# Gate logits with stationary weights in four column quarters, v moved past them, and the result turned by VectorE

## The chip, the core and the metric

One NeuronCore of a Trainium2 chip. The metric is the device time of one execution in microseconds (us). An engine is called PE (TensorE's matmuls), PEld (its weight loads), DVE (VectorE), ACT (ScalarE), POOL (GpSimd) or SP (SyncE) in the profile. Runs of one batch share a chip and are compared with the same runs of the kernel before. A ratio and its 95% interval are against the kernel before in the same batch.

## The reference, cut to what matters

```python
B, H, S, D = 8, 8, 576, 64                       # batches, heads, positions, head size
attn = exp(scores + bias) / sum                  # causal
x = (attn @ v) -> (B, S, H*D)                    # 512 columns a token
logits = einsum('bsd,de->bse', x, w_gate)        # 8 experts
local  = einsum('bsd,de->bse', x, w_local)       # 1 more column
# a token takes its argmax expert, or keeps the one of the token before (local gate)
h = relu(x @ w1[e]);  out = p[e] * (h @ w2[e])   # 8 experts, 512 -> 1024 -> 512
```

The kernel does not wait for x to get the gate logits. It computes v times the gate weights (nine columns a head) for each pair of heads, puts the result beside v, and lets the value rows of the attention carry these columns along. The rows then give x, its logits and the softmax sum in one product.

## The kernel before

The attention loop has 32 iterations, one for each pair of heads. All matmuls are fp32. The parts that the change touches, with cuts marked:

```python
HW = DH + E + 1                 # 73
VW = 2 * HW + 2                 # 148: sum | logits, v of head 0 | v, logits of head 1 | sum
TAIL = 2 * VW                   # banks are PSUM banks of 512 columns
GATE = TAIL + TL
gates = banks[1][:, GATE : GATE + NB * 2 * (E + 1)].rearrange("p (c h e) -> p c h e", c=NB, h=2)

def tail_scores(n):
    for h in range(2):
        d = slice(DH * h, DH * h + DH)
        mm(banks[1][d, TAIL : TAIL + TL], lhsT=ins[n][1][:, TS:][:, d], rhs=ins[n][0][:, TS:], ...)

def gate_parts(n):              # v stationary, the weights (18 columns) moving
    m = P // 2
    for c in range(NB):         # 5 chunks of positions
        for j in range(0, P, m):
            mm(gates[j : j + m, c], lhsT=ins[n][2][:, c * P + j : c * P + j + m], rhs=wz[:, n % HP], ...)

def beside_v(n):
    v = ins[n][3]
    nc.vector.tensor_copy(v[:, :, 1 : E + 2], gates[:, :, 0])
    nc.vector.tensor_copy(v[:, :, VW - E - 2 : VW - 1], gates[:, :, 1])

def rows(n, g):                 # ... scores stationary, v moving; then the division by the sums
    ...
# one iteration of the loop
    scores(n, u); weights(n, piece); tail(n); seen_tail(n)      # cut
    rows(n - 1, 1)
    rows(n - 1, 0)
    tail_scores(n + 1)
    gate_parts(n)
    beside_v(n)
```

In the expert stage, two early blocks of x are turned on TensorE, `transpose(ps[:, c, :], x[:, 128 columns], ident)` four times a block.

## Time and profile before

| | before |
|---|---|
| time, median of 4 runs | 789.76 us (788.81 to 790.12) |
| PE busy | 98% of the span |
| clean iteration of the attention loop | 6.93 us |
| of it: 10 logit matmuls | about 0.57 us |

The page, the clean iteration, the chain and the timeline stand in the prediction below. A clean iteration is one in which PE doesn't stop and nothing but the loop's own work is issued to it. What remains is what the logits' group and its two copies look like in the groups by form. The columns are: line, engine, operation, output from inputs, partitions by columns, count | busy us, mean ns of one | idle time of the engine before them.

```profile
L370 PE MATMUL o<-wz,vt 128*64 128x18 f32 x640 | 24.7, 209 | 0.6 <-issue 0.6
L375 DVE COPY v<-o 128x45 f32<-128x45 f32 x32 | 6.4, 199 | 8.1 <-PE o L370 4.2 <-DMA v<-in_vx_dram 2.9 <-PE bank L972 0.7
L376 DVE COPY v<-o 128x45 f32<-128x45 f32 x32 | 6.2, 195 | 0.0
```

The logits are 640 rows, 20 an iteration, because an fp32 matmul shows as two passes. Their mean of 209 ns is latency, not cost: 20 of them start within 0.57 us.

### The profile page before, as it was taken

How to read it: one execution, taken by the hardware profiler on the slowest of the kernel's cores; microseconds unless marked ns; L12 is line 12 of the kernel's file. 1: busy time of each engine (PE TensorE's matmuls, PEld its weight loads, DVE VectorE, ACT ScalarE, POOL GpSimd, SP SyncE). 2: the span in 40 equal slices, each digit the busy share in tenths (PEclk: the TensorE clock that was granted, in tenths of full speed). 3: DMA queues.
4: the chain of work that ended last, by engine and by line, in shares of the span. 5: the costliest groups of instructions: out<-in, count | busy, mean ns of one | idle time of the engine just before them, and what ended most of it. 6: DMA issues, size and time to landing. Idle time of an engine off the chain costs nothing.

```text
span 798.9 us, 18230 instructions
## 1 busy us (share of the span) xinstructions
PE 783.0 (98%) x7078; PEld 561.8 (70%) x7078; DVE 338.4 (42%) x1228; ACT 237.0 (30%) x611; POOL 175.4 (22%) x329
## 2 busy tenths in 40 slices
PE   9999999999999989999999999999999999999996
PEld 8989888888888854853777547774577735676762
DVE  3234444454557649325462264522655226546000
ACT  5767766756664111111111111111111111111110
POOL 3422344455432241101210002101111011011001
PEclk9999999999999999999999999999999999999999
DMA  9485579877474389956999369993699946994001
GB/s 312 170 294 186 187 236 303 312 247 237 170 254 179 113 290 411 393 192 242 335 387 408 127 228 352 387 395 116 246 345 394 361 150 229 373 411 188 22 14 43
DMA packets 64145, 204.47 MB, mean 256 GB/s; under 512 B 8269, under 2 KB 8301, under 8 KB 64048
## 3 DMA queue, kind: packets, MB, share of 16 engines
q1 hardware_dynamic: 55008, 172.41, 60.2%
q0 software_dynamic: 8896, 30.47, 10.0%
q8 instruction: 58, 0.95, 0.5%
q14 instruction: 39, 0.32, 0.1%
q10 hardware_dynamic: 144, 0.33, 0.1%
HBM read 179.93 MB, written 23.76 MB: 255 GB/s over the span
## 4 chain that ended last, share of the span: by engine, by line
issue 59%; PE 30%; POOL 4%; DVE 2%; POOLq 1%; SPq 1%; another core or an unknown queue 1%; DMA 0%; DVEq 0%
PE o L408 13%; PE ps L330 11%; POOL out_dram L1249 2%; PE o L370 2%; POOL xg L1184 2%; PE hp L1231 2%; PE o L286 1%; POOLq L1159 1%; PE o L351 1%; SPq L808 1%; PE bank L947 1%; DVE xT L1088 0%; SPq L804 0%; DVE x L413 0%
## 5 line engine op out<-in xcount | busy, mean ns | idle before, releaser
L1088 DVE STREAM_TRANSPOSE xT<-xg 32x128 f32<-32x128 f32 x576 | 174.2, 302 | 173.3 <-PE hp L1231 97.1
L1244 PE MATMUL yp<-w,hT 128*128 128x512 f32 (+1 forms) x528 | 217.6, 595 | 0.0
L1231 PE MATMUL hp<-xT,w 128*128 128x256 f32 (+1 forms) x1088 | 193.0, 337 | 2.8 <-issue 2.5
L1231 PEld LDWEIGHTS hp<-xT,w 128*128 128x128 f32 x1088 | 172.2, 191 | 27.4 <-issue 11.0
L339 ACT ACTIVATE sc<-ps,bias 128x256 f32<-128x256 f32 (+3 forms) x448 | 156.5, 482 | 60.6 <-PE ps L330 58.6
L1244 PEld LDWEIGHTS yp<-w,hT 128*128 128x128 f32 (+1 forms) x528 | 90.7, 181 | 115.4 <-issue 114.5
L1249 POOL DMA_INDIRECT out_dram<-y,at_gate x38 | 38.5, 1012 | 439.9 <-ACT y L1248 425.4
L408 PE MATMUL o<-v,sc 128*64 128x74 f32 x3072 | 117.9, 229 | 3.1 <-issue 2.9
L408 PEld LDWEIGHTS o<-v,sc 128*64 128x64 f32 x3072 | 110.9, 136 | 11.8 <-issue 9.2
L1235 ACT ACTIVATE hT<-hp 128x512 f32<-128x512 f32 x68 | 40.4, 597 | 195.6 <-PE hp L1231 183.3
L1248 ACT ACTIVATE y<-yp,at_gate 128x512 f32<-128x512 f32 x38 | 26.1, 688 | 240.5 <-PE yp L1244 234.3
L345 POOL TENSOR_SCALAR_AFFINE_SELECT sc<-sc 128x256 f32<-128x256 f32 x160 | 66.5, 420 | 129.0 <-ACT sc L339 60.8
L330 PE MATMUL ps<-q,k 64*128 64x320 f32 (+2 forms) x768 | 92.3, 386 | 0.0
L330 PEld LDWEIGHTS ps<-q,k 64*128 64x128 f32 x768 | 69.6, 186 | 14.6 <-ACT r_v L957 0.6
L1244 PE MATMUL yp<-x,hT 128*128 128x512 f32 (+1 forms) x144 | 63.3, 594 | 0.0
L1222 DVE STREAM_TRANSPOSE hT<-x 32x256 f32<-32x256 f32 x64 | 27.9, 436 | 65.4 <-ACT x L1216 64.5
L410 DVE RECIPROCAL recs<-o 128x4 f32<-128x4 f32 x64 | 12.1, 189 | 92.0 <-PE o L408 80.3
L1231 PEld LDWEIGHTS hp<-xT,x 128*128 128x128 f32 x320 | 46.1, 191 | 5.8 <-issue 2.6
L1231 PE MATMUL hp<-xT,x 128*128 128x128 f32 (+1 forms) x320 | 50.1, 317 | 0.0
L1244 PEld LDWEIGHTS yp<-x,hT 128*128 128x128 f32 (+1 forms) x144 | 25.3, 178 | 26.2 <-issue 25.8
L1038 POOL DMA_INDIRECT x_rows<-x,r_slot_i x40 | 38.9, 973 | 9.3 <-issue 5.7
L413 DVE TENSOR_TENSOR x<-o,recs 128x292 f32<-128x292 f32 x64 | 34.5, 538 | 2.2
(163 smaller groups left out, 350.6 us busy)
## 6 DMA issues: line engine op xcount, KB each, us to landing
w<-in_w_dram SPq DMA_DIRECT2D x184, 512.0 KB
x<-in_w_dram SPq DMA_DIRECT2D x56, 512.0 KB
v<-in_vx_dram SPq DMA_DIRECT2D x32, 370.0 KB
vt<-in_vz_dram SPq DMA_DIRECT2D x32, 320.0 KB
k<-in_kz_dram SPq DMA_DIRECT2D x31, 320.0 KB
q<-in_q_dram SPq DMA_DIRECT2D x32, 288.0 KB
xg<-x_rows POOLq DMA_DIRECT2D x30, 293.0 KB
x_rows<-r_empty SPq DMA_DIRECT2D x6, 293.0 KB
```

Source lines behind the costliest of these rows:

```text
L330: mm(ps[:, h, at : at + z - a], lhsT=kb[d, c * P : c * P + P], rhs=qb[d, a:z], start=True, stop=True)
L339: nc.scalar.activation(scs[n, u][:, h, at : at + z - a], raw[u][:, h, at : at + z - a], Act.Exp, bias=bias[:, i : i + 1], scale=scale)
L345: nc.gpsimd.affine_select(out=x, in_=x, compare_op=Alu.is_ge, fill=0.0, base=0, pattern=[[0, 2], [1, P]], channel_multiplier=-1)
L408: mm(y, lhsT=w, rhs=x, start=start, stop=stop)
L413: nc.vector.tensor_tensor(x, y, rec.unsqueeze(3).to_broadcast([P, t1 - t0, 2, HW]), op=Alu.mult)
L1038: self.s.nc.gpsimd.indirect_dma_start(out=next(self.s.views)[:, :], out_offset=bass.IndirectOffsetOnAxis(ap=self.slot[:z, m : m + 1], axis=0),
L1088: self.nc.vector.transpose(self.xT[i][d : d + m, :, k * P + a * m : k * P + a * m + m], rows[a * m : a * m + m, :, X0 + d : X0 + d + m])
L1222: nc.vector.transpose(hT[i][d : d + m, :, a : a + m], x[a : a + m, :, d : d + m])
L1231: mm(y, lhsT=w[0][:, c, f : f + P], rhs=xT[i][:, c, :], start=(c == 0), stop=(c == DK - 1))
L1235: nc.scalar.activation(hT[i][:, g : g + per], ps, Act.Relu)
L1244: mm(ps[n * m : n * m + m, :], lhsT=hT[i][:, c, a : a + m], rhs=wn[:, c, :], start=(c == 0), stop=(c == FK - 1))
L1249: nc.gpsimd.indirect_dma_start(out=next(outs)[:, :], out_offset=bass.IndirectOffsetOnAxis(ap=at[i, k][:, 0:1], axis=0), in_=y[:, :], eleme ...
```

## The change

Intent: with v stationary, ten matmuls load 64 columns each to multiply 18. Turned round, the weights (32 columns, of which 18 are not zero) are stationary, and v's positions move past them. The array is used as four quarters of 32 columns, each with its own 32-position slices of the five chunks (5x32 = 160 moving columns), so four matmuls do what ten did. The result comes out with logits on partitions; VectorE turns it in 32x32 squares into a slot of 32 columns between the two heads' v.

```diff
+SLOT = 32
+VX = 2 * DH + SLOT + 2
+PARTS = slice(0, VW // 2), slice(VX - VW // 2, VX)
@@
-    TAIL = 2 * VW
-    GATE = TAIL + TL
+    scores_of_tail = banks[0][:, 3 * VW : 3 * VW + TL]
+    gates = banks[1][:, 2 * VW : 2 * VW + NB * SLOT].rearrange("p (c n) -> p c n", c=NB)
@@ def gate_parts(n):
-        m = P // 2
-        for c in range(NB):
-            for j in range(0, P, m):
-                mm(gates[j : j + m, c], lhsT=ins[n][2][:, c * P + j : c * P + j + m], rhs=wz[:, n % HP],
-                   start=True, stop=True)
+        m = P // 4
+        v = ins[n][2].rearrange("p (c n) -> p c n", c=NB)
+        for j in range(0, P, m):
+            mm(gates[j : j + m], lhsT=wz[:, n % HP], rhs=v[:, :, j : j + m], start=True, stop=True)
@@ def beside_v(n):
-        nc.vector.tensor_copy(v[:, :, 1 : E + 2], gates[:, :, 0])
-        nc.vector.tensor_copy(v[:, :, VW - E - 2 : VW - 1], gates[:, :, 1])
+        nc.vector.transpose(ins[n][3][:, :, 1 + DH : 1 + DH + SLOT], gates)
@@ the loop
             rows(n - 1, 1)
+            divide(n - 1, 1)
             rows(n - 1, 0)
         if n + 1 < NPAIR:
             tail_scores(n + 1)
+        if n:
+            divide(n - 1, 0)
@@ def product (x turned by TensorE in the experts)
-            self.nc.tensor.transpose(ps[:, c, :], x[:, 2 * c * HW + X0 : 2 * c * HW + X0 + P], self.ident)
+            for h in range(2):
+                self.nc.tensor.matmul(ps[h * DH : h * DH + DH, c, :], lhsT=rows[:, c, X0[h] : X0[h] + DH],
+                                      rhs=self.ident, start=True, stop=True)
... (cut: the layout of v and x in memory, the stores that follow it, the weights' slot, gx 5 -> 4)
```

The logits now take 160 columns of the second bank. With the rows' 296 and the tail's 64 that is 520, more than the bank's 512. So the tail's scores had to move to the first bank, and that bank's division had to move behind them.

More of the change, by code (lines that the diff above doesn't have):

```diff
@@ L33 @@
 VW = 2 * HW + 2
+SLOT = 32
+VX = 2 * DH + SLOT + 2
+PARTS = slice(0, VW // 2), slice(VX - VW // 2, VX)
 TOPS = ((0, None), (1, 2), (4, 3), (5, 6), (8, 7))
 PLAIN = ((0, 1), (2, 3), (4, 5), (6, 7), (8, None))
-X0 = E + 1
+X0 = 0, 2 * HW - DH
 XI = H * HW
@@ L197, in general @@
                     r0, z = b * S + t * P, min(P, S - t * P)
-                    nc.sync.dma_start(xb[:z, t, :XI].rearrange("p (a w) -> p a w", w=2 * HW)[:, :, X0 : X0 + P],
-                                      x_d[r0 : r0 + z, :].rearrange("p (a w) -> p a w", w=P))
+                    for h in range(2):
+                        nc.sync.dma_start(xb[:z, t, :XI].rearrange("p (a w) -> p a w", w=2 * HW)[:, :, X0[h] : X0[h] + DH],
+                                          x_d[r0 : r0 + z, :].rearrange("p (a w) -> p a w", w=P)[:, :, h * DH : h * DH + DH])
                 g = sort.group((b,), {b: xb})
@@ L252, in load @@
         ins[n] = [p_in.tile([P, S], F32, name="q"), *(p_in.tile([P, TS + 2 * TL], F32, name=x) for x in ("k", "vt")),
-                  p_vx.tile([P, NB, VW], F32, name="v")]
+                  p_vx.tile([P, NB, VX], F32, name="v")]
         for t, x, eng in zip(ins[n], (q[b][:, hp], kz[n], vz[n], vx[n]), (nc.sync, other, nc.sync, nc.sync)):
@@ L268, in attention @@
     load(2)
-    wz = keep.tile([P, HP, 2, E + 1], F32, name="wz")
+    wz = keep.tile([P, HP, SLOT], F32, name="wz")
     nc.gpsimd.memset(wz, 0.0)
@@ L273, in attention @@
         d = slice(h * DH, h * DH + DH)
-        for w, a, z in ((w_gate, 0, E), (w_local, E, E + 1)):
-            nc.gpsimd.dma_start(wz[d, :, h, a:z], w.rearrange("(a h d) e -> h d a e", h=2, d=DH)[h])
+        at = 0 if h == 0 else SLOT - E - 1
+        for w, a, z in ((w_gate, at, at + E), (w_local, at + E, at + E + 1)):
+            nc.gpsimd.dma_start(wz[d, :, a:z], w.rearrange("(a h d) e -> h d a e", h=2, d=DH)[h])
     seen = once.tile([P, TL], F32, name="seen")
@@ L350, in tail_scores @@
             d = slice(DH * h, DH * h + DH)
-            mm(banks[1][d, TAIL : TAIL + TL], lhsT=ins[n][1][:, TS:][:, d], rhs=ins[n][0][:, TS:], start=True, stop=True)
+            mm(scores_of_tail[d], lhsT=ins[n][1][:, TS:][:, d], rhs=ins[n][0][:, TS:], start=True, stop=True)
     def tail(n):
@@ L356, in tail @@
         i = tail_bias + n
-        nc.scalar.activation(sc, banks[1][:, TAIL : TAIL + TL], Act.Exp, bias=bias[:, i : i + 1], scale=scale)
+        nc.scalar.activation(sc, scores_of_tail, Act.Exp, bias=bias[:, i : i + 1], scale=scale)
     def seen_tail(n):
@@ L361, in seen_tail @@
         nc.vector.scalar_tensor_tensor(x, x, 3e38, seen, Alu.min, Alu.mult)
-    gates = banks[1][:, GATE : GATE + NB * 2 * (E + 1)].rearrange("p (c h e) -> p c h e", c=NB, h=2)
     def gate_parts(n):
-        m = P // 2
-        for c in range(NB):
-            for j in range(0, P, m):
-                mm(gates[j : j + m, c], lhsT=ins[n][2][:, c * P + j : c * P + j + m], rhs=wz[:, n % HP],
-                   start=True, stop=True)
+        m = P // 4
+        v = ins[n][2].rearrange("p (c n) -> p c n", c=NB)
+        for j in range(0, P, m):
+            mm(gates[j : j + m], lhsT=wz[:, n % HP], rhs=v[:, :, j : j + m], start=True, stop=True)
     def beside_v(n):
-        v = ins[n][3]
-        nc.vector.tensor_copy(v[:, :, 1 : E + 2], gates[:, :, 0])
-        nc.vector.tensor_copy(v[:, :, VW - E - 2 : VW - 1], gates[:, :, 1])
+        nc.vector.transpose(ins[n][3][:, :, 1 + DH : 1 + DH + SLOT], gates)
     def rows(n, g):
-        b, hp = divmod(n, HP)
-        if (b, "x") not in xs:
-            xs[b, "x"] = new_x(b)
         t0, t1 = COLUMNS[g]
@@ L391, in rows @@
                 y = ps[half * TL : half * TL + TL, t - t0]
-                last = i * TL == TS
-                if last:
-                    todo[half].append((y, scs[n, "tail"], v[:, NF], True, False))
                 cs = range(min(i // 2 + 1, NF))
-                for h in range(2):
-                    d = slice(h * VW // 2, (h + 1) * VW // 2)
+                for h, d in enumerate(PARTS):
+                    out = y[:, h * VW // 2 : (h + 1) * VW // 2]
+                    last = i * TL == TS
+                    if last:
+                        todo[half].append((out, scs[n, "tail"], v[:, NF, d], True, False))
                     for c in cs:
@@ L401, in rows @@
                         at += i * TL - a
-                        todo[half].append((y[:, d], scs[n, u][:, h, at : at + TL], v[:, c, d], not last and c == 0,
-                                           c == cs[-1] and (h == 1 or not last)))
+                        todo[half].append((out, scs[n, u][:, h, at : at + TL], v[:, c, d], not last and c == 0,
+                                           c == cs[-1]))
         while any(todo):
@@ L408, in rows, with divide @@
                     mm(y, lhsT=w, rhs=x, start=start, stop=stop)
+    def divide(n, g):
+        b, hp = divmod(n, HP)
+        if (b, "x") not in xs:
+            xs[b, "x"] = new_x(b)
+        t0, t1 = COLUMNS[g]
+        ps = banks[g][:, : (t1 - t0) * VW].rearrange("p (t w) -> p t w", w=VW)
         rec = recs[:, n, 2 * t0 : 2 * t1].rearrange("p (t h) -> p t h", h=2)
@@ L419, in logits @@
             pair = keep.tile([P, NF, HP, E + 1], F32, name="pair")[:m, : t1 - t0]
-            nc.vector.tensor_tensor(pair, part[:, :, :, : E + 1], part[:, :, :, 2 * HW - E - 1 :], op=Alu.add)
+            nc.vector.tensor_tensor(pair, part[:, :, :, DH:HW], part[:, :, :, HW : HW + E + 1], op=Alu.add)
             nc.vector.tensor_reduce(lg[:m, b * NB + t0 : b * NB + t1, :], pair.rearrange("p t a e -> p t e a"),
@@ L1088, in squares @@
                 self.nc.vector.transpose(self.xT[i][d : d + m, :, k * P + a * m : k * P + a * m + m],
-                                         rows[a * m : a * m + m, :, X0 + d : X0 + d + m])
+                                         rows[a * m : a * m + m, :, X0[d // DH] + d % DH :][:, :, :m])
     def product(self, i, k, n, x, ps):
@@ L1094, in product @@
         ps = ps.rearrange("p (c n) -> p c n", c=DK)
+        rows = x[:, :XI].rearrange("p (c w) -> p c w", w=2 * HW)
         for c in range(DK):
-            self.nc.tensor.transpose(ps[:, c, :], x[:, 2 * c * HW + X0 : 2 * c * HW + X0 + P], self.ident)
+            for h in range(2):
+                self.nc.tensor.matmul(ps[h * DH : h * DH + DH, c, :], lhsT=rows[:, c, X0[h] : X0[h] + DH], rhs=self.ident,
+                                      start=True, stop=True)
         self.nc.vector.tensor_copy(self.xT[i][:, :, k * P : k * P + P], ps)
@@ L1132, in experts @@
     ps_r = pool("ps_r", 3, space=PSUM)
-    gx = gx or pool("gx", 5)
+    gx = gx or pool("gx", 4)
     ws, xg = (ready["w"], ready["x"]) if ready else ({}, {})
@@ L1321 @@
     kz, vz = (_np.zeros((NPAIR, 2, DH, TS + 2 * TL), _np.float32) for _ in range(2))
-    vx = _np.zeros((NPAIR, P, NB, VW), _np.float32)
+    vx = _np.zeros((NPAIR, P, NB, VX), _np.float32)
     for h in range(2):
@@ L1327 @@
         x = v[:, h::2].reshape(NPAIR, S, DH)
-        some = vx[:, :, :, h * (VW // 2) :][..., : VW // 2]
-        some = some[..., E + 2 :], some[..., 0], some[..., :DH], some[..., VW // 2 - 1]
-        some = some[2 * h : 2 * h + 2]
+        some = vx[..., (1, VX - 1 - DH)[h] :][..., :DH], vx[..., (0, VX - 1)[h]]
         some[0][:, :, :NF] = x[:, :TS].reshape(NPAIR, NF, P, DH).transpose(0, 2, 1, 3)
```

## The prediction

> **What bounds the kernel now.** I read the page's busy shares first, then the busy time by stage, the costliest groups, the order of work inside one iteration of the attention loop, and last the list of waits.
>
> ```profile
> PE 783.0 (98%) x7078; PEld 561.8 (70%) x7078; DVE 338.4 (42%) x1228; ACT 237.0 (30%) x611; POOL 175.4 (22%) x329
> ...
> L408 PE MATMUL o<-v,sc 128*64 128x74 f32 x3072 | 117.9, 229 | 3.1 <-issue 2.9
> ```
>
> TensorE is busy for 98% of the span and no other engine for half of it. The change touches the first 256 us, the attention loop of 32 iterations (one per pair of heads). One undisturbed iteration, from the windows view:
>
> ```profile
> 63.77:70.70 6.93, 6.93 (x149) 6.29 (x147) 2.04 (x8) 5.00 (x15) 2.04 (x5) 1.00 0.61 198
> ```
>
> The columns after the length are the busy times of PE, PEld, DVE, ACT and POOL, then clock and DMA. PE is busy for all 6.93 us, ACT for 5.00, DVE and POOL for 2.04. So in a clean iteration a PE microsecond saved is a microsecond saved. What an iteration's PE time consists of, from the chain of work in order of time:
>
> ```profile
> 42.05 2.79 PE ps L330 x24
> 44.84 3.42 PE o L408 x95
> 48.25 0.05 PE o L351
> ...
> 48.43 0.55 PE o L370 x19
> 48.98 2.98 PE ps L330 x24
> ```
>
> Scores (L330) take 2.79 us, the value rows (L408) 3.4, the tail's scores (L351) 0.1 and the logit parts (L370, the target of this change) about 0.57. Their ends and starts, from the timeline of PE around the logits:
>
> ```profile
> 62.96 0.23 PE L408 MATMUL o<-v,sc 128*64 128x74 f32 x1
> 63.01 0.23 PE L351 MATMUL o<-q,k 128*64 128x64 f32 x2
> 63.06 0.20 PE L370 MATMUL o<-wz,vt 128*64 128x18 f32 x1
> 63.08 0.22 PE L351 MATMUL o<-q,k 128*64 128x64 f32 x1
> 63.11 0.74 PE L370 MATMUL o<-wz,vt 128*64 128x18 f32 x19
> 63.77 0.54 PE L330 MATMUL ps<-q,k 64*128 64x320 f32 x2
> ```
>
> An fp32 matmul shows as two matmul rows and two weight loads (10 in the source, 20 here). From the last tail matmul's start (63.08) to the first scores matmul (63.77) pass 0.69 us: this stretch is what the change rewrites. A row's printed length (0.2 us) is latency; successive starts give the cost. The 20 logit passes start over 0.57 us in two column halves, 10 per half, so 57 ns per pass of only 18 moving columns: they are held by the loading of 64 stationary columns, not by streaming.
>
> **Rates that I use.** The page's groups by form give the streaming rate and an example of switching the array's shape:
>
> ```profile
> L1244 PE MATMUL yp<-w,hT 128*128 128x512 f32 x432 | 189.2, 595 | 0.0
> 359.57 0.59 PE L1244 MATMUL yp<-w,hT 128*128 128x512 f32 x1
> 360.10 0.65 PE L1214 MATMUL hp<-w,xT 128*64 128x512 f32 x2
> ```
>
> 189.2/432 = 438 ns per pass of 512 columns, or 0.84 ns a column in steady steps of 0.43 us. From the full array to column halves the step is 0.53 us, so a change of shape costs about 0.10 us. And the first two matmuls of the halves (x2) span 0.65 us together, one alone being about 0.64: both halves stream at once, although the second follows the two passes of the first in program order. The halves work independently of each other.
>
> **What the Trainium skill says.** "TensorEngine Tiling (Array Packing)", Key Properties: changing the tiling mode drains TensorE, and tiles load and multiply independently; the trace agrees, with the 0.10 us and the paired starts. Its tables list 128 by 32 as four tiles; no row of the kernel before shows four at once with fp32. "TensorE: Matmul & The Clock Gate", LDWEIGHTS: loading costs columns/1.2 ns whatever the rows, so 53 ns for 64 columns (trace: 57 per pass) and, as an estimate from that page, 27 ns for 32. The same page, Measured speedup vs the span model, gives 2.38x for three column tiles; whether that carries to fp32 passes is the main uncertainty. "PSUM — Partial Sum Buffer", PSUM bank collisions: two engines must not use one bank and quadrant together, so dependencies are kept by bank; the trace has such a wait, of the tail's scores for the division that reads other columns of the same bank:
>
> ```profile
> PEld o L351 <- DVE x L413: 1.7, 6, 0.3
> ```
>
> **The change, part by part.**
>
> (1) Logits. Removed per iteration: 10 matmuls (20 passes, 64 stationary columns, 18 moving). Added: 4 matmuls (8 passes, 32 stationary columns in four column quarters, 5x32 = 160 moving). If the quarters run at once, each does two passes of 160 x 0.84 = 135 ns. Counting from the last tail matmul: its own streaming of 64 columns 0.055, a new change of shape (halves to quarters) 0.10, one exposed load 0.027, two passes 0.27, stagger of the starts 0.02, then the change of shape to the scores 0.10 that was paid before as well: 0.57 us against 0.69. I take 0.13 us saved per iteration, times 31 full iterations: -4.0 us. The instructions fall by far more than the time: the new moving columns and the extra change of shape eat most of it.
>
> (2) Value rows. The tail's matmul of 148 columns becomes two of 74, since the heads' columns are no longer adjacent. In the first group that half of the array has now 16 matmuls of 74 instead of 14 and one of 148; the other half has 16 already. Same columns streamed: 0 us.
>
> (3) VectorE. Two copies of 128x45 (about 0.2 us each) become one 128x160 transpose. The existing 128-element transposes take 302 ns; I estimate 0.35 us for 160 columns. Its result is needed one iteration later, after 2.79 us of scores: 0 us on the path.
>
> (4) Tail's scores go from the second bank to the first, and the division of the first bank comes after them. The wait of 1.7 us in six iterations moves to the logits, some 0.3 us later (tail matmuls and a change of shape lie between), about as long as the longest such wait. Each of those iterations also loses the overlap of tail and logits. Most of it goes: -1.2 us.
>
> (5) Experts. Two blocks of x are turned on TensorE by four transposes each, between matmuls of the first layer:
>
> ```profile
> 263.49 0.60 PE L1096 MATMUL bank<-ident,xg 128*128 128x128 f32 x4
> 263.92 0.60 PE L1231 MATMUL hp<-xT,w 128*128 128x256 f32 x2
> ```
>
> 263.49 to 263.92 in this timeline, so 0.44 us a block. They become 8 ordinary fp32 matmuls with two passes of 128 columns, in two column halves: 4 x 2 x 0.109 = 0.87 us, plus two changes of shape and exposed loads of about 0.3. That is +0.7 us a block, +1.4 us in all, on a PE that has no gap there. The expert stage's VectorE transposes keep their shape and count.
>
> (6) Transfers. v grows from 148 to 162 columns, 370 to 405 KB per iteration. DMA's share in a clean iteration is 0.61 and loads are issued three iterations ahead: 0.
>
> Sum: -4.0 - 1.2 + 1.4 = -3.8, from 790.0 to about 786.2 us.
>
> **Rivals.**
>
> *Quarters do not run four at once.* For it: the trace shows only two fp32 streams together. If two quarters share, the passes take 4 x 135 = 0.54 us instead of 0.27 and each iteration loses 0.14: 31 x 0.14 = +4.3, with (4) and (5) about 794.5. If all eight passes are serial, 1.08 us, each loses 0.68: some +21 us, 811. Against it: the two halves show no loss at all from sharing. I give the first 10%, the second 3%.
>
> *Quarters do not drain after halves.* If only the row side of the shape matters, the extra 0.10 us falls away: 3 us better, 783. For it, nothing in the trace: all visible changes of shape cost it. 15%.
>
> *The saving is swallowed by a wait that takes its place.* Iterations 13 to 30 are longer than 6.93 us (up to 8.5); there PE stops inside the rows while GpSimd issues the scatters, by 0.2 to 0.6 us at a time. These stops are put down to "issue", not to a semaphore of ACT or GpSimd. If they are latency from scores to rows through ACT and GpSimd, up to half of the saving in those iterations goes, 1.5 us. Against it: in them ACT still waits for the scores. If they are instructions arriving late, fewer PE instructions (20 of nearly 300 per iteration) help slightly. The same holds for a stop of about 3 us near 287 us, with a low clock after it (0.73 in that window), where ACT stands still: a shift of timing can make it larger or smaller by two or three microseconds. That widens the range both ways.
>
> *VectorE becomes the bound, or the expert stage does not start earlier.* VectorE has 4.9 us free per clean iteration. The expert stage's second weights land by 263 us and are first needed near 271: 8 us of slack. I give neither weight.
>
> **Range and chances.** Centre 786.2. Three microseconds either way cover the change of shape, the moved wait and the stops; the two-at-once rival lies outside above. 80% range 781.5 to 791. Faster by over 2% needs 774.2 or less, four times the expected gain: 0.02. Slower by over 2% needs 805.8, only the serial rival: 0.04. Within 2%: 0.94.
>
> **What will show it.** In the profile after: logit rows of 128*32 and 128x160, 256 in all, with four starts within some 20 ns and the next four about 0.135 us on; a gap of 0.57 us between the last tail matmul and the first scores matmul; a clean iteration of about 6.80 us; one 0.35 us transpose per iteration; no wait of the tail's scores for the division; 1.1 us per turned block in the experts. Wrong if the quarters' starts come one pair at a time (6.93 or more per iteration), if the gap falls to about 0.47 (no drain), or if the clean iterations gain and the end of the attention loop, now at 255 us, does not move by 5 us.

## The result, and the profile after

| | before | after |
|---|---|---|
| median | 789.76 us (788.81 to 790.12, 4 runs) | 784.06 us (783.42 to 784.55, 4 runs) |
| ratio | | 0.9929, 95% interval 0.9912 to 0.9946 |

Executions over 1.5% slower than the fastest of the same kernel are left out of the means. Ratios are the mean time of one kernel's runs over that of the other's runs of the same rounds, so they are not quite the ratio of the medians. (In the experiments they come out when the first round, which was profiled, is left out.) The change is 0.7% faster, inside the class "within 2%".

The busy shares on the page of the changed kernel:

```profile
PE 773.0 (99%) x6782; PEld 546.2 (70%) x6782; DVE 339.0 (43%) x1196; ACT 237.2 (30%) x611; POOL 176.2 (23%) x329
```

Its clean iteration in the windows view:

```profile
62.64:69.44 6.80, 6.80 (x140) 5.87 (x137) 2.08 (x7) 5.00 (x15) 2.04 (x5) 1.00 0.68 199
```

PE has 296 rows fewer and still fills the iteration; the iteration is 0.13 us shorter (6.930 to 6.796 from the records' starts). The groups by form of the logits and of the turning:

```profile
L374 PE MATMUL o<-vt,wz 128*32 128x160 f32 x256 | 15.7, 311 | 0.0
L377 DVE STREAM_TRANSPOSE v<-o 128x160 f32<-128x160 f32 x32 | 10.9, 342 | 2.8 <-DMA v<-in_vx_dram 2.8
```

256 rows in place of 640, and one turning of 342 ns in place of two copies of 199 and 195 ns. The timeline around them (start us, length us):

```profile
62.01 0.29 PE L356 MATMUL o<-q,k 128*64 128x64 f32 x3
...
62.23 0.48 PE L374 MATMUL o<-vt,wz 128*32 128x160 f32 x8
62.36 0.20 DVE L416 RECIPROCAL recs<-o 128x6 f32<-128x6 f32 x1 [0.72 <-PE o L356]
62.64 2.86 PE L335 MATMUL ps<-q,k 64*128 64x320 f32 x24
63.12 0.34 DVE L377 STREAM_TRANSPOSE v<-o 128x160 f32<-128x160 f32 x1
```

PE goes from the tail's scores (L356) to the logits (L374) to the next scores (L335) without a stop. The last tail matmul of the three starts at 62.08, so the stretch that the prediction counted is 0.56 us, against 0.69 before. The division of the first bank (L416) now waits for the tail's scores (L356), on VectorE, which has time. The turning ends at 63.46, two microseconds before PE leaves the scores. Each record of the eight logit passes has a start:

```
us: 62.231 62.238 62.245 62.251 | 62.391 62.398 62.405 62.411
```

Four start within 20 ns. The records don't name the quarter, but a quarter's pass of 160 columns takes 0.135 us, so these four are in four quarters and stream at once. The second passes follow 0.160 us later, not the 0.135 us that the prediction expected; the 0.025 us are about the one exposed weight load of its sum. The experts' turned block:

```profile
250.38 1.09 PE L1107 MATMUL bank<-ident,xg 128*64 128x128 f32 x16
251.40 3.72 PE L1243 MATMUL hp<-xT,w 128*128 128x256 f32 x16
```

From its start to the next layer's start 1.02 us pass, against 0.44 before; the work on both sides of it loses another 0.2 to the changes of shape.

**The profile of before was of a bad execution.** Its execution took 800.54 us, ten more than the timed runs (1.49% above the fastest of them), so its end of attention (255 us) can't be held against 242 us here. It shows stops of this kind in the rows of iterations 13 to 30 (timeline of PE):

```profile
234.47 0.63 PE L408 MATMUL o<-v,sc 128*64 128x74 f32 x10 [0.35 <-issue]
```

And it has a stretch near 287 us in which PE works for 3.55 of 6 us at a mean granted clock of 0.73 (windows view):

```profile
286.00:292.00 6.00, 3.55 (x6) 1.70 (x6) 2.95 (x20) 1.57 (x3) 0.96 (x1) 0.73 0.63 193
```

The first experiment therefore took a second profile of the same kernel.

### The profile page after: what moved, and what is told of

Its sections match the earlier page's. It is cut to its first block, busy times and chain, and to the rows that moved or that the text cites. A ratio compares the mean times of both kernels' runs of the same rounds, so it can differ in the third digit from the quotient of the medians.

```text
span 782.4 us, 17629 instructions
## 1 busy us (share of the span) xinstructions
PE 773.0 (99%) x6782; PEld 546.2 (70%) x6782; DVE 339.0 (43%) x1196; ACT 237.2 (30%) x611; POOL 176.2 (23%) x329
## 4 chain that ended last, share of the span: by engine, by line
issue 58%; PE 32%; POOL 5%; DVE 2%; POOLq 2%; DMA 1%; DVEq 0%
PE o L406 14%; PE ps L335 11%; POOL out_dram L1261 2%; POOL xg L1196 2%; PE hp L1243 2%; PE o L374 2%; PE o L291 1%; POOLq L1171 1%; DMA x_rows<-x,r_slot_i 1%; PE o L356 1%; PE bank L956 0%; DVE xT L1097 0%; POOL x_rows L1047 0%; PE bank L1107 0%; PE bank L981 0%
## 5 line engine op out<-in xcount | busy, mean ns | idle before, releaser
L406 PE MATMUL o<-v,sc 128*64 128x74 f32 x3072 | 113.6, 228 | 0.8 <-issue 0.8
L406 PEld LDWEIGHTS o<-v,sc 128*64 128x64 f32 x3072 | 108.8, 136 | 8.1 <-issue 4.3
L335 PE MATMUL ps<-q,k 64*128 64x320 f32 (+2 forms) x768 | 92.5, 386 | 0.1
L335 PEld LDWEIGHTS ps<-q,k 64*128 64x128 f32 x768 | 68.9, 186 | 20.0 <-issue 4.8
L416 DVE RECIPROCAL recs<-o 128x4 f32<-128x4 f32 x64 | 12.1, 189 | 87.0 <-PE o L406 63.1
```

The source lines that it names most:

```text
L335: mm(ps[:, h, at : at + z - a], lhsT=kb[d, c * P : c * P + P], rhs=qb[d, a:z], start=True, stop=True)
L406: mm(y, lhsT=w, rhs=x, start=start, stop=stop)
```

## The experiments

### Both kernels again: before_again, after_again

No edit; the two kernels as they are.

> The kernel before once more, with a second profile. Ratio 1.000. The profile in hand spans 798.9 us although the timed runs take 790: if its stops inside the rows (iterations 13 to 30), the waits of the tail's scores and the stop near 287 us belong to that one execution, this profile spans about 788 us and most of them are gone; if they belong to the kernel, it spans 799 again with the same stops. Clean iterations 6.93 us either way.

> The changed kernel once more, for a tighter ratio: 0.993, some 5.6 us. Sum known from the traces so far: 31 iterations x 0.134 us saved = -4.2, turning of x in the experts +1.4, so -2.8; the other -2.8 is open. Clean iterations 6.80 us again.

Measured: before 789.07 us (787.24 to 790.26, ratio 1.0004, interval 0.9990 to 1.0017); after 783.71 us (783.42 to 784.68, ratio 0.9933, interval 0.9919 to 0.9946). The expectation for before held: the profiled execution is now 787.24 us, with a span of 785.5 us and a clock of 1.00 in both windows below. Up to 252 us the bad profile had 13 stops of PE of over 0.15 us; up to 243 us this one has two, 0.52 us at 57.0 and 0.66 us at 242.3. Windows of before up to the first expert layer, and from there to the end:

```profile
0.00:246.15 246.15, 243.08 (x4836) 217.89 (x4836) 111.66 (x414) 164.27 (x494) 105.11 (x241) 1.00 0.74 243
246.15:785.50 539.35, 532.57 (x2243) 341.14 (x2243) 226.56 (x816) 72.53 (x117) 69.57 (x88) 1.00 0.72 268
```

The same of after:

```profile
0.00:241.99 241.99, 239.00 (x4516) 204.67 (x4516) 112.81 (x382) 164.27 (x494) 105.17 (x241) 1.00 0.75 252
241.99:782.50 540.51, 533.99 (x2267) 341.97 (x2267) 226.50 (x816) 72.51 (x117) 69.53 (x88) 1.00 0.72 267
```

So clean against clean, attention gains 4.2 us, the experts lose 1.2 us (539.35 to 540.51), and 3.0 us remain. The timed medians of that batch differ by 5.45 us (789.16 over nine runs of before, to 783.71), the fastest runs by 3.61 (787.03 to 783.42). The runs of before spread over 3 us and those of after over 1.3. A typical run of before takes 1.9 us more than its profiled one (787.24), a typical run of after 0.5 us less than its own (784.17); these 2.4 us of the gain are in neither profile, and no kept profile shows a typical run of before.

### The tail's scores moved, nothing else: tail_moved

```diff
-    TAIL = 2 * VW
-    GATE = TAIL + TL
+    scores_of_tail = banks[0][:, 3 * VW : 3 * VW + TL]
+    GATE = 2 * VW
...
+            divide(n - 1, 1)
             rows(n - 1, 0)
...
             tail_scores(n + 1)
+        if n:
+            divide(n - 1, 0)
```

> The kernel before with part 4 of the change alone: the tail's scores in the first bank, the division of the first bank after them; logits as before. Theory (the moved wait supplies the open 2.8 us): 1.5 to 3 us faster, ratio 0.9962 to 0.998, no wait of the tail's scores for the division, clean iterations still 6.93 us. Rival (the open part comes from fewer TensorE instructions to fetch, 20 of 300 per iteration): ratio 1.000.

Measured: 790.34 us (787.94 to 790.66), ratio 1.0010, interval 0.9997 to 1.0024. The theory fell: the move gains nothing by itself. Its clean iteration, in the windows view:

```profile
64.01:70.94 6.93, 6.93 (x149) 6.29 (x147) 2.04 (x8) 4.99 (x15) 2.03 (x5) 1.00 0.63 195
```

It is that of the kernel before to the hundredth. The waits of the tail's scores for the division are absent here, but they are absent in the second profile of before as well. They belonged to the bad execution, not to the kernel.

The move even has a small price, in the list of waits: the scores' weight loads wait for the routing's ranks (`r_rank`), which VectorE works out after the divisions. The three lines are of before_again, tail_moved and the changed kernel (us in total, times, longest):

```profile
PEld ps L330 <- DVE r_rank L1006: 0.5, 2, 0.3
...
PEld ps L330 <- DVE r_rank L1014: 1.3, 4, 0.4
...
PEld ps L335 <- DVE r_rank L1015: 1.6, 4, 0.5
```

Counted from one first scores matmul to the next, with the first iteration as 0, iterations 13, 21, 25 and 29 of tail_moved are each 0.13 us longer than those of before_again.

### The same turned product in two halves: halves

The weights stand in a slot of 96 columns with zeros on both sides, so that a 64-column half takes two accumulating matmuls, one for each of its quarters. All else is as in the changed kernel.

```diff
-    wz = keep.tile([P, HP, SLOT], F32, name="wz")
+    wz = keep.tile([P, HP, 3 * SLOT], F32, name="wz")
...
-            mm(gates[j : j + m], lhsT=wz[:, n % HP], rhs=v[:, :, j : j + m], start=True, stop=True)
+            first = j % (2 * m) == 0
+            some = wz[:, n % HP, SLOT:] if first else wz[:, n % HP, : 2 * SLOT]
+            mm(gates[j // (2 * m) * 2 * m :][: 2 * m], lhsT=some, rhs=v[:, :, j : j + m], start=first, stop=not first)
```

> The changed kernel with the logits' weights in two column halves (64 stationary columns, the other 32 of them zero, two accumulating matmuls of 160 columns per half): as many instructions as the quarters, no change of shape after the tail, but each half streams four passes of 160 columns. Theory (the gain comes from four streams at once): from the last tail matmul to the first scores matmul about 0.71 us instead of 0.56, clean iterations 6.95 us, 31 x 0.15 = 4.7 us slower than the changed kernel, about 788.7, ratio to the kernel before 0.999. Rival (the gain comes from fewer instructions): as fast as the changed kernel, ratio 0.993.

Measured: 788.87 us (788.78 to 789.63), ratio 0.9999, interval 0.9986 to 1.0013; the expected time and ratio held, and the rival fell, since halves has as many rows of PE as the changed kernel (6782) and gains nothing. The logits in the timeline:

```profile
62.66 0.76 PE L376 MATMUL o<-vt,wz 128*64 128x160 f32 x8
```

The clean iteration in the windows view:

```profile
63.36:70.34 6.99, 6.99 (x138) 6.15 (x137) 2.08 (x7) 4.99 (x15) 2.03 (x5) 1.00 0.65 198
```

The same number of logit matmuls, the same columns moved, two at a time: 6.99 us (expected 6.95), longer than before, and 0.75 us from the last tail matmul to the first scores matmul (expected 0.71). In this form, turning the operands round does not gain by itself; the gain is that four stream at once. Also, from the first tail matmul to the first logits pass 0.235 us here and 0.329 in the changed kernel: going from halves to quarters costs about 0.09 us.

### Each logits matmul two and three times: doubled, thrice, thrice_mixed

The result stays right, since each overwrites the same value.

```diff
-        for j in range(0, P, m):
+        for j in [j for j in range(0, P, m) for _ in range(2)]:      # doubled: 0,0,1,1,2,2,3,3
+        for j in [j for j in range(0, P, m) for _ in range(3)]:      # thrice:  0,0,0,1,1,1,...
+        for j in [j for _ in range(3) for j in range(0, P, m)]:      # thrice_mixed: 0,1,2,3,0,1,2,3,...
```

> The changed kernel with each of the four logits matmuls issued twice, the result the same. If four quarters stream at once, each quarter has four passes of 0.14 us instead of two: 0.28 us per iteration, 32 x 0.28 = 9.0 us, so 792.7 us, with the narrow spread of the changed kernel (about 1 us over its runs). If the quarters were served in turn, 8 more passes of 0.14: 36 us, 820. Theory for the open 2.4 us (the number of TensorE instructions brings stops that vary from run to run): with 16 more instructions per iteration it has nearly as many as the kernel before, so runs spread over 3 us and the median is near 795.

> The changed kernel with each of the four logits matmuls issued three times: 0.56 us per iteration, 17.9 us, 801.6 us if only streaming counts; if the number of TensorE instructions brings stops, more than the kernel before has now, so some 3 us above that and a wide spread.

> The changed kernel with each of the logits' four matmuls issued three times, as in the earlier run that came to 827.2 us, but with the quarters taken in turn (0,1,2,3,0,1,2,3,0,1,2,3) instead of each quarter's three together. If the order in which the quarters are issued is what kept them from overlapping there, each group of four passes adds 0.146 us as in the doubled run (0.292 us for two groups), so four groups more add 0.58 us an iteration: clean iteration 7.38 us, 783.7 + 31 x 0.58 = 801.8 us (800 to 803), and the four quarters' first passes start within 0.02 us. If it is the number of passes of the stage, the iteration stays at 8.2 us and the time at 827 us.

Measured: doubled 792.80 us (792.33 to 794.11, ratio 1.0056); thrice 827.20 us (827.15 to 827.82, ratio 1.0489); thrice_mixed 802.32 us (801.75 to 802.39, ratio 1.0149). The first came in where streaming puts it, and not where the theory of the instruction count did (795 us and a spread of 3 us; it was 1.8). The second missed both expectations by 23 to 26 us, and the third, which was made to find out why, came in at the sum for an overlap of four. Starts of the logit passes in one iteration, in us, from the records of each trace:

```
doubled       63.972 .986 .999 64.012 | 64.132 .146 .159 .172 | 64.268 ... | 64.404 ...     (16 starts in 0.47 us)
thrice        63.956 64.116 .252 .257 .387 .417 .523 .553 .559 .659 ... 65.428 65.564       (24 starts in 1.61 us)
thrice_mixed  58.966 .973 .979 .986 | 59.126 .133 .139 .146 | 59.262 ... | 59.398 ... (24 starts in 0.72 us)
```

The timeline shows the same as one row of each. Thrice first, then thrice_mixed:

```profile
63.96 1.91 PE L374 MATMUL o<-vt,wz 128*32 128x160 f32 x24
```

```profile
58.97 1.02 PE L374 MATMUL o<-vt,wz 128*32 128x160 f32 x24
```

The same 24 passes take 1.91 us when a quarter's three matmuls stand together, and 1.02 us when the quarters take turns. In doubled, four passes of a quarter stand together and the quarters still start together, each later-issued quarter ahead of the first quarter's second matmul. In thrice, six stand together, and the next quarter's first pass starts only as the first quarter's third one has started: at 63.956, 64.257, 64.559 and 64.861, 0.30 us apart. The order of issue is thus what ended the overlap, not the count. One reading fits all three rows of starts: a quarter takes up at most four passes, the running one among them, and when one more is due for it, all that were issued later wait too. In thrice there is room for the fifth and sixth pass when the second and third start, and 5 ns after the third (64.252) the next quarter begins (64.257). This is argued, not shown. That TensorE looks four passes ahead in the order of issue does not fit: in doubled the thirteenth pass starts 40 ns after the first. The changed kernel has two passes of a quarter in a row and lies on the safe side.

### The division ahead of the tail's scores: divide_first

```diff
+            divide(n - 1, 0)
             tail_scores(n + 1)
-        if n:
-            divide(n - 1, 0)
```

> The changed kernel with the division of the first bank ahead of the tail's scores, which now write that bank: the tail's scores wait for two VectorE instructions (0.20 and 0.61 us and the start of the first, 0.2 us after the last row matmul). About 0.95 us per iteration, 31 of them: 29 us slower, 813 us, and PEld of the tail's scores waits for the division in every iteration. If the order did not matter: 783.7.

Measured: 819.99 us (819.02 to 820.19), ratio 1.0392, interval 1.0373 to 1.0410: slower, by more than expected. The wait in the list of waits (us in total, times, longest):

```profile
PE o L356 <- DVE x L419: 28.1, 30, 0.9
```

One of its thirty in the timeline:

```profile
60.39 0.20 DVE L416 RECIPROCAL recs<-o 128x6 f32<-128x6 f32 x1 [0.59 <-PE o L406]
60.62 0.61 DVE L419 TENSOR_TENSOR x<-o,recs 128x438 f32<-128x438 f32 x1
61.28 0.34 PE L356 MATMUL o<-q,k 128*64 128x64 f32 x4 [0.94 <-DVE x L419]
```

PE stands for 0.94 us in 30 iterations until the division of the bank has been read. The iteration grows by 1.16 us (6.796 to 7.955), from the last row's start (60.120) to the tail's first (61.284) alone 1.16 us; the printed wait is shorter because it is counted from the printed end of the last row, whose latency otherwise lies under the next matmuls. So with the tail's scores in the first bank, the division's place behind them is what keeps the move free.

### The experts' early blocks turned by VectorE: dve_turn, one_turn

The part of the change that costs, both blocks turned by TensorE in 16 passes each, is given to VectorE, for both blocks or for the second alone.

```diff
-        turn_x(1, 0, True)
+        turn_x(1, 0)            # dve_turn only
         layer1(0, 4, FK - 2)
-        turn_x(1, 1, True)
+        turn_x(1, 1)            # dve_turn and one_turn
```

> The changed kernel with the two early blocks of x in the experts turned by VectorE instead of TensorE. TensorE is rid of twice 1.2 us: 781.3 us if VectorE, which needs 16 x 0.3 = 4.8 us per block, is in time for the second expert's first layer; a wait of TensorE for the turned x of up to several us, and no gain or a loss, if not.

> The changed kernel with only the second of the two early blocks of x turned by VectorE; the first stays with TensorE. If the earlier run with both on VectorE lost because VectorE's thirty-two squares of the first block pushed the routing's work back, so that TensorE waited for it (1.2 us for the one-hot rows, 2.5 us at the next matmul), then with one block on VectorE that wait is shorter or gone: the second turning (1.1 to 1.2 us of TensorE) is saved and the time is 782.5 to 783.2 us. If any work put on VectorE there is waited for, the time is 784.5 to 787 us, as with both.

Measured: dve_turn 786.95 us (785.40 to 787.82), ratio 0.9979, interval 0.9963 to 0.9996, so some 3 us slower than the changed kernel (783.71 in the batch before). One_turn 785.08 us (784.15 to 785.46), ratio 0.9929, interval 0.9908 to 0.9950: as the changed kernel, with no gain. The interval is 3.3 us wide and the expected gain about 1, so the traces have to decide. From the first expert layer to the end they show 540.51 us for after_again, 541.31 for one_turn and 542.57 for dve_turn: VectorE's turning loses. (A block takes 16 squares, not the thirty-two of the expectation.) In one_turn's timeline:

```profile
257.01 5.04 DVE L1097 STREAM_TRANSPOSE xT<-xg 32x128 f32<-32x128 f32 x16
...
260.68 0.60 ACT L1247 ACTIVATE hT<-hp 128x512 f32<-128x512 f32 x1 [4.30 <-PE hp L1243]
...
262.15 1.10 PE L1243 MATMUL hp<-xT,w 128*128 128x256 f32 x4 [1.50 <-ACT hT L1247]
```

The 16 squares of a block take VectorE 5.04 us and end at 262.05; PE goes on at 262.15. The profile puts the wait of 1.50 us down to ACT, but ACT had ended at 261.28: PE waited for the squares. The 1.2 us that TensorE saves go into that stop. With both blocks on VectorE, dve_turn, the list of waits has a second one, for the routing's one-hot rows that stand behind the first block's squares on VectorE:

```profile
PE hp L1243 <- issue: 2.5, 1, 2.5
...
PE bank L1002 <- DVE r_hot L991: 1.2, 1, 1.2
```

None of these runs beats the changed kernel.

## Why the prediction was right

It said 786.2 us, 781.5 to 791.0, within 2%; measured 784.06. The mechanism of the logits was right, one step of the sum failed (step 4), and nearly half of the measured gain is in no step.

- **Step 1, logits, -0.13 us by 31 iterations: right in the clean iteration.** It went from 6.930 to 6.796 us, -0.134, which would be -4.2 us over 31 of them; what came of it over the loop is told below. Each part of the sum shows: the stretch of 0.57 us is 0.56; four quarters start within 20 ns, so the overlap carried over to fp32 passes in full; successive groups of four are 0.136 us apart in steady state (doubled, thrice_mixed), as 160 columns at 0.84 ns gave; the change from halves to quarters costs about 0.09 us. Rival one (two at a time, 794.5 us) and the serial one fall with the halves and the starts; rival two (no change of shape to pay) falls with the 0.56 us. The halves show that the operands' turning alone would have given nothing.
- **Step 2, rows, 0: right.** From the first row to the first tail matmul a clean iteration takes 3.26 us before and 3.27 us after.
- **Step 3, VectorE, 0: right in the clean iteration.** 342 ns instead of the estimated 350, and it ends inside the scores. But in four iterations the scores wait for VectorE's routing work (1.6 us in all, against 0.5 before; lines under tail_moved).
- **Step 4, the tail's scores' bank, -1.2: wrong.** Moved alone, it changed nothing (ratio 1.0010). The wait of 1.7 us that the step wanted to remove was read from an execution ten microseconds slower than the timed ones; a second profile of the same kernel does not have it. The step's own number was taken as a property of the kernel when it was a property of one execution. The move was needed for room in the bank, and it is nearly free only with the division behind it (about 4 by 0.13 us in tail_moved): ahead of it, +36 us.
- **Step 5, experts, +1.4: right.** From 0.44 us to 1.02 us a block plus 0.2 us for the changes of shape on either side; that is 0.8 us for the first block; the stage as a whole loses 1.2 us, so the second loses some 0.4.
- **Step 6, transfers, 0: right.** In the changed kernel's list of waits only two weight loads of the rows wait for a transfer, 0.2 us each.

Without step 4 the sum is -2.6, close to the -3.0 us between the two clean profiles, and part of that is luck. Counted from one first scores matmul to the next (the first iteration is 0), before_again less after_again, most iterations gain 0.13 us and some 0.25. Iterations 13, 21, 25 and 29, in which the scores wait for VectorE, lose 0.06 to 0.14. And 0.85 us of the gain come from iterations 6 and 7 of before_again, around one stop (timeline of PE):

```profile
57.04 0.53 PE L370 MATMUL o<-wz,vt 128*64 128x18 f32 x11 [0.52 <-issue]
```

The 31 iterations gain 4.28 us with it and 3.43 without, where 31 clean savings would be 4.15. So the third rival, a wait in place of the saving, came true for some 0.7 us, by VectorE and not by ACT or GpSimd.

The measured medians differ by 5.45 to 5.7 us, nearly twice what the clean profiles show. The other 2.5 us or so are in no step: step 4's -1.2, which failed, only brought the sum nearer to the result. The prediction named stops put down to "issue" as a cause of width and not of gain, and its range covered them. That the 2.5 us are such stops is argued, not shown. The two profiles of after (784.02 and 784.17 us, typical runs) have none of over 0.15 us in the loop but one of 0.8 us in its last iteration, where before_again has one of 0.66.

A hint at what such stops wait for stands in the packed records of the traces. In before_again, tail_moved, one_turn and thrice_mixed, there are eight of them (0.19 to 1.01 us) before the last iterations of the loop. Each ends 1.3 to 1.6 us after a 16 KB packet of the DMA queue "q8 instruction" has landed, though such packets come only every 6 us or so. This speaks for instructions that arrive late, but no run tests it, and the stops of the bad execution mostly do not keep this distance. The count of PE's instructions does not decide alone: halves (6782 rows of PE) spreads over 0.9 us and tail_moved (7078 rows) over 2.7, but doubled (7038) over 1.8, and thrice and thrice_mixed (7294 each) over under 0.7, although thrice_mixed's profile has three of the eight stops.

The prediction's end-of-attention test, 5 us earlier, could not be judged on the first pair of profiles; clean against clean it is 4.2. Two of its readings are slightly off without consequence: 0.69 less 0.57 is 0.12 and not the 0.13 that it took, and the longest iteration in its profile took 9.04 us, not 8.5.

## What to carry to other kernels

Count what TensorE streams and how many tiles of the array stream at once: fewer, wider matmuls gain only by the part that runs side by side, and the issue order must let the tiles take turns. Before a wait from a profile enters a sum, compare that execution's own time with the timed runs, and profile once more where it is an outlier. When work leaves a full engine, look at what waits for it in its new place: a saving of 1.2 us on TensorE was lost to a stop of 1.5 us for VectorE's slower turning.

## What the Trainium skill lacked or had wrong

- "TensorE: Matmul & The Clock Gate", The mechanism (what overlaps and what doesn't), says that matmuls are in strict order in start and end. Here, as far as starts go (ends in a trace are modelled), later-issued matmuls of another column quarter start first: in doubled, the other quarters' first passes start 14 to 40 ns after the first quarter's, whose own second matmul comes 0.30 us after it.
- No page has how many passes of one tile may stand together before the overlap of tiles ends: with four in a row 16 passes started within 0.47 us, with six in a row 24 passes within 1.61 us, and with the quarters taking turns 24 within 0.72 us.
- "TensorEngine Tiling (Array Packing)", Key Properties, says that a change of mode drains the engine, but not what it costs: about 0.09 us from halves to quarters here.
- No page has how far the runs of one kernel on one core differ: 787.03 to 792.26 us for the kernel before over all batches, and one profiled execution at 800.54.
